# Two second products moved ahead of a kv product, and one x product moved ahead of an h product, in a fused attention and feed-forward kernel

## The chip, the cores and the metric

One core of a Trainium2 chip. The metric is the device time of one execution in microseconds (us), median over executions. Every position below is in us from the start of the profiled execution of the kernel named. The engines are called PE (matmuls; PEld are its weight loads), ACT (ScalarE), DVE (VectorE), POOL (GpSimd) and SP (issues most DMAs). The granted clock is the share of PE's full clock that it was given. All timed runs quoted are "fast" (here: not over 1.5% above the fastest run of the same kernel), apart from one single run.

## The reference, cut to what matters

```python
# q, k, v: 8 batches, 8 heads, 576 positions, 64 wide
q_s = softmax(q, axis=-1); k_s = softmax(k, axis=2)
kv   = einsum('bhsd,bhse->bhde', k_s, v)        # "kv product"
x    = einsum('bhsd,bhde->bhse', q_s, kv)       # "x product", 4608 x 512 in all
h = x @ w_in                                    # "h product", 512 -> 2048
s = sin(alpha * h)
g = h + s * s / (alpha + 1e-09)
out = g @ w_out                                 # "second product", 2048 -> 512
```

## The kernel before

Tokens go through in nine blocks t of 512; a batch has 576 tokens, so the attention of later batches is woven between the products of earlier blocks. On each engine instructions run in the order of the program. An h product is four matmuls (L248), a second product's step is one (L268), each 512 columns wide. `take(os, n)` issues the next n second-product matmuls. The first place of the change is in batch 1:

```python
        cast_v(1, [ACT_CP, DVE_CP])      # v to bf16: first half on ACT, second on DVE
        exp_to(A["qe", 1][:, 7:J], q78)
        take(os, 3)
        kv_mm(1, 0, ps_e, split=True)    # first kv product: needs v's first half
        kv_norm(1, 0, 1)
        take(os, 3)
        kv_mm(1, 1, ps_e, split=True)
        kv_norm(1, 1, 2)
        take(os, 1)
        ...                              # two x products, each followed by take(os, 2)
        take(os)                         # what is left of the 64
        ...                              # then the h products of t=1
```

The second is in block t=2, whose h products carry the attention of batch 3 between them:

```python
    def attn_out(b, ii, half, pool, eng):            # one x product and its copy to xT
        ...
        xp = pool.tile([128, 2, 512], F32, name="xp", tag="a")   # pool ps_a: one buffer
        for e in range(2):
            nc.tensor.matmul(xp[:, e, 0:n], kt[:, e, ii], qT[...], start=True, stop=True)
        c0 = (J * b + j0) * P
        eng(xT[:, 2 * ii:2 * ii + 2, c0:c0 + n], xp[:, :, 0:n])

    def attn_back(b, n, engs=(DVE_CP, DVE_CP), xs=(4, 6, 8, 10)):
        if n == 0:
            ...                                      # the kv products of batch b
        elif n in xs:
            m = xs.index(n)
            attn_out(b, m // 2, m % 2, ps_a, engs[m % 2])
    ...
    for ni in range(nN):                             # 16 h products
        h_slot(2, ni, SQ2[ni], lag, lent)            # h product, sine (ACT), square (ACT or POOL)
        flush(lag, 2)                                # g (DVE), two behind
        attn_back(3, ni - 5, (DVE_CP, ACT_CP), (5, 7, 9, 10))
```

I call the h products h0 to h15, and batch 3's four x products x0 to x3. They follow h10, h12, h14 and h15; x0 and x2 are copied by DVE, x1 and x3 by ACT, and all four use one PSUM buffer (PSUM holds what matmuls write; the pool `ps_a` has one tile of it).

The softmax here doesn't subtract the row's maximum and nothing guards it: scores larger than these inputs give would overflow.

Of the kernel before, what the change touches and what calls it, by code (L numbers as in the profile page):

```python
# [23 lines left out]
def kernel(  # L24
# [52 lines left out]
    def src_view(t, b):  # L77
        return t[b].rearrange("(i e) (p j) d -> (e p) i (j d)", e=2, j=J)
# [7 lines left out]
    def load(name, t, b, halves=False, eng=nc.sync, gate=None):  # L86

        st = stage.tile([128, 4, J, D], F32, name=f"st_{name}", tag="st")
        for ii in range(2) if gate else ():
            gate(st[:, ii, 0, 0:1], zero)  # L90
        view = src_view(t, b)
        flat = st.rearrange("p i j d -> p i (j d)")
        if halves:
            for ii in range(2):
                eng.dma_start(out=flat[:, ii::2], in_=view[:, ii::2])
        else:
            eng.dma_start(out=flat, in_=view)
        staged[name, b] = st

    def load_batch(b):  # L100
        load("q", q, b)
        load("k", k, b)
        load("v", v, b)
# [6 lines left out]
    def load_wout(c):  # L110
        nc.gpsimd.dma_start(out=wout[:, 4 * c:4 * c + 4, :], in_=wout_v[:, 4 * c:4 * c + 4, :])
# [4 lines left out]
    def exp_to(dst, src, iis=range(2)):  # L116
        for ii in iis:
            nc.scalar.activation(dst[:, :, ii * 128:(ii + 1) * 128].rearrange("p j (x d) -> p x j d", x=2),  # L118
                                 src[:, ii::2], AX.Exp)
# [5 lines left out]
    def exp_half(name, b, ii, j1=J):  # L125
        if ii == 0:
            A[name + "e", b] = att2.tile([128, J, 4 * D], BF16, name=name + "e")
        exp_to(A[name + "e", b][:, 0:j1], staged[name, b][:, :, 0:j1], (ii,))

    def exp_k(b):  # L130
        A["ke", b] = att2.tile([128, J, 4 * D], BF16, name="ke")
        exp_to(A["ke", b], staged["k", b])
# [22 lines left out]
    def norm_late(b, j0):  # L155

        qe = A["qe", b][:, j0:J].rearrange("p j (i d) -> p j i d", i=4)
        qs = small.tile([128, J, 4], F32, name="qs")[:, j0:J]
        nc.vector.tensor_reduce(qs, qe, axis=AXL.X, op=ALU.add)
        nc.vector.reciprocal(qs, qs)  # L160
        nc.vector.tensor_tensor(qe, qe, qs.unsqueeze(3).to_broadcast([128, J - j0, 4, D]), op=ALU.mult)
# [25 lines left out]
    def q_tile(b):  # L187
        if ("qT", b) not in A:
            A["qT", b] = att2.tile([128, 2, J, 128], BF16, name="qT")
        return A["qT", b]  # L190
# [6 lines left out]
    def q_transpose_ii(b, ii, j0, j1, tp):  # L197

        for j in range(j0, j1):
            nc.tensor.transpose(tp[:, j - j0], A["qn", b][:, ii, j], identb)  # L200
# [24 lines left out]
    def attn_chunk(b, c, j0, j1, xp):  # L225

        ii, e = divmod(c, 2)
        nc.tensor.matmul(xp, kbd[b % 2][:, e, ii], A["qT", b][:, ii, j0:j1, e * 64:(e + 1) * 64],
                         start=True, stop=True)
# [51 lines left out]
    ACT_CP, DVE_CP, GP_CP = nc.scalar.copy, nc.vector.tensor_copy, nc.gpsimd.tensor_copy  # L281
# [4 lines left out]
    def load0(eng, n, t, ii, j0=0, j1=J):  # L286
        eng.dma_start(out=staged[n, 0][:, ii::2, j0:j1].rearrange("p i j d -> p i (j d)"),
                      in_=src_view(t, 0)[:, ii::2, j0 * D:j1 * D])
# [80 lines left out]
    def h_slot(t, ni, sq, lag, wide=None):  # L369
        hp = mm_h(t, ni, wide, 2 if t < 2 and ni < 2 else 0)  # L370
        lag.append((t, ni, hp, sine(t, ni, hp, sq)))

    def flush(lag, keep):
        while len(lag) > keep:
            combine(*lag.pop(0))

    def o_quad(t, accs, engs):

        R = range(4)
        by_m, by_n = [(n, m) for m in R for n in R], [(n, m) for n in R for m in R]  # L380
        orders = [by_m, by_n, by_n, by_m]
        for c in R:
            for n, m in orders[c]:
                mm_o(t, m, 4 * c + n, accs[m])
                if c == 3 and n == 3:
                    evac_o(t, m, accs[m], engs[m])
                yield

    def take(it, n=1000):
        for _ in range(n):  # L390
            if next(it, 0) == 0:
                return
# [4 lines left out]
    with ES:  # L397
        def lent():
            return ps_e.tile([128, 2, MF], F32, name="hh", tag="a")[:, 0]

        def load_q8():
            for ii in range(2):
                load0(nc.sync, "q", q, ii, 8, 9)

        def load_q1():
            staged["q", 1] = st = stage.tile([128, 4, J, D], F32, name="st_q", tag="st")
            for ii in range(2):
                DVE_CP(st[:, ii, 0, 0:1], zero)
            for ii in range(2):
                nc.sync.dma_start(out=st[:, ii::2, 0:7].rearrange("p i j d -> p i (j d)"),  # L410
                                  in_=src_view(q, 1)[:, ii::2, 0:7 * D])

        late = {4: load_q8, 6: load_q1, 8: lambda: load_wout(2),
                10: lambda: load_wout(3), 13: lambda: load("k", k, 1, halves=True, gate=DVE_CP)}
        for ni in range(nN):
            h_slot(0, ni, "DPPAPPAPPPAPPAPP"[ni], lag, lent)
            flush(lag, 1)
            if ni in late:
                late[ni]()
        flush(lag, 0)  # L420

        accs = [ps_h.tile([128, dm], F32, name="hp", tag="h") for _ in range(4)]
        os = o_quad(0, accs, [DVE_CP, ACT_CP, DVE_CP, DVE_CP])
        take(os, 46)
        exp_to(A["qe", 0][:, 8:9], staged["q", 0][:, :, 8:9])
        for ii in range(2):
            exp_half("q", 1, ii, 7)
        load("v", v, 1, halves=True)
        nc.sync.dma_start(out=q78.rearrange("p i j d -> p i (j d)"), in_=src_view(q, 1)[:, :, 7 * D:J * D])
        load_batch(2)  # L430
        norm_late(0, 8)
        norm_q(1, [GP, V], 7)
        exp_k(1)
        q_tile(1)
        for ii in range(2):
            tp = ps_e.tile([128, 16, 128], BF16, name="tp", tag="a")
            q_transpose_ii(1, ii, 0, 7, tp)
            if ii == 1:
                for i2 in range(2):
                    nc.tensor.transpose(tp[:, 8 + i2], A["qe", 0][:, 8, i2 * 128:(i2 + 1) * 128], identb)  # L440
            DVE_CP(A["qT", 1][:, ii, 0:7], tp[:, 0:7])
        DVE_CP(A["qT", 0][:, :, 8], tp[:, 8:10])
        take(os, 6)
        xp = ps_e.tile([128, 4, P], F32, name="xp", tag="a")
        for c in range(4):
            attn_chunk(0, c, 8, 9, xp[:, c])
        DVE_CP(xT[:, :, 8 * P:9 * P], xp)
        cast_v(1, [ACT_CP, DVE_CP])
        exp_to(A["qe", 1][:, 7:J], q78)
        take(os, 3)  # L450
        kv_mm(1, 0, ps_e, split=True)
        kv_norm(1, 0, 1)
        take(os, 3)
        kv_mm(1, 1, ps_e, split=True)
        kv_norm(1, 1, 2)
        take(os, 1)

        c0 = J * P
        for ii in range(2):
            xp = ps_e.tile([128, 2, 512], F32, name="xp", tag="a")[:, :, 0:7 * P]  # L460
            for e in range(2):
                attn_chunk(1, 2 * ii + e, 0, 7, xp[:, e])
            (ACT_CP, DVE_CP)[ii](xT[:, 2 * ii:2 * ii + 2, c0:c0 + 7 * P], xp)
            if ii == 0:
                nc.scalar.activation(zero, zero, AX.Sin)
            take(os, 2)
        take(os)
        norm_late(1, 7)
        load("q", q, 3)
        load("k", k, 3)  # L470

        for ki in range(2):
            for ni in range(2):
                mm_h(1, ni, lent, ki, ki + 1)
        for ni in range(nN):
            h_slot(1, ni, SQ[ni], lag, lent)
            flush(lag, 1)
        cast_v(2, [GP_CP, GP_CP])
        flush(lag, 0)
# [17 lines left out]
    os = o_stream(1)  # L497
# [40 lines left out]
    def attn_back(b, n, engs=(DVE_CP, DVE_CP), xs=(4, 6, 8, 10)):  # L538
        if n == 0:
            kv_mm(b, 0, ps_a)  # L540
            kv_mm(b, 1, ps_a)
            kv_norm(b)
# [3 lines that stand above are left out]
# [5 lines left out]
    for ni in range(nN):  # L551
        h_slot(2, ni, SQ2[ni], lag, lent)
        flush(lag, 2)
        attn_back(3, ni - 5, (DVE_CP, ACT_CP), (5, 7, 9, 10))
    flush(lag, 0)

    for t in range(3, nT):
        b = t + 1 if t + 1 < B else None
        os = o_stream(t - 1)
# [59 lines left out]
```

## Time and profile before

| | before |
|---|---|
| median of 6 runs | 287.76 us (287.33 to 288.11) |
| profiled execution | span 285.8 us, granted clock 0.999 |
| PE busy | 95% of the span |
| PE's starts around the first kv product of batch 1 | 41.27, then 42.09 |
| h products of t=1 begin | 46.14 |
| from the first g of t=2 to h4 of t=3 | 21.95 us |

How to read it: the chain of waits says which engine's work ended last at each moment; where it is on PE, only fewer or earlier matmuls help; where it is on another engine, PE is waiting for it. The last row is a ruler. It is taken from the timelines of DVE and PE (columns: start, duration, engine, line, operation, tiles, shape, count, idle time before and what ended it). Its first end in the profile of before is this row; its other end is the h product at 103.23 that the prediction shows:

```profile
81.28 2.75 DVE L264 SCALAR_TENSOR_TENSOR g<-s,inva_sb,hp 128x512 bf16<-128x512 f32 x4
```

The ruler frees the second place of the change from whatever happened earlier in the same execution: 103.23 - 81.28 = 21.95.

### The profile page before, as it was taken

The numbers are of one execution on the slowest core, as the hardware profiler recorded it, in microseconds if no ns is written. First come the engines' busy times: TensorE is split into PE (matmuls) and PEld (weight loads), VectorE is DVE, ScalarE is ACT, GpSimd is POOL, SyncE is SP. The second block draws the span as 40 slices with busy tenths as digits, with TensorE's granted clock in tenths as the row PEclk, the third lists the DMA queues.
The fourth block names the chain that finished last, engine by engine and source line by source line (L and its number), as shares of the span: only waits on it lengthen the run. The fifth ranks groups of instructions, "written<-read, shape, count | busy, mean of one in ns | idle before, by whom it ended". The sixth has DMA issues, their size and how long they took to land.

```text
span 285.8 us, 4247 instructions
## 1 busy us (share of the span) xinstructions
PE 272.6 (95%) x1541; PEld 130.8 (46%) x1569; DVE 192.6 (67%) x291; ACT 226.0 (79%) x321; POOL 80.6 (28%) x75
## 2 busy tenths in 40 slices
PE   2899999999999999999999999999999999999994
PEld 1444454445454454444544454445444444444443
DVE  4857967999999658766785677667674555555321
ACT  4898748999489999899889988998877777777400
POOL 2869512773477480005300530041000000000000
PEclk9999999999999999999999999999999999999999
DMA  7999999843999984139711990016011111111242
GB/s 261 308 204 243 260 397 407 312 169 78 275 222 412 372 169 105 37 69 406 218 38 39 359 292 20 22 36 155 1 39 37 37 37 39 37 38 41 46 100 73
DMA packets 38581, 45.77 MB, mean 160 GB/s; under 512 B 16528, under 2 KB 22432, under 8 KB 38560
## 3 DMA queue, kind: packets, MB, share of 16 engines
q1 hardware_dynamic: 33376, 40.57, 46.3%
q0 software_dynamic: 4992, 4.79, 9.7%
q8 instruction: 12, 0.20, 0.3%
q10 hardware_dynamic: 192, 0.14, 0.2%
q14 instruction: 9, 0.07, 0.1%
HBM read 36.71 MB, written 9.44 MB: 161 GB/s over the span
## 4 chain that ended last, share of the span: by engine, by line
PE 74%; DVE 9%; DMA 7%; ACT 4%; issue 3%; POOL 2%; SPq 0%; ACTq 0%
PE op L268 33%; PE hp L248 33%; DMA st_v<-in_v_dram 5%; ACT s L254 3%; DVE g L264 2%; POOL s L258 2%; PE kvp L171 2%; DVE qs L150 2%; PE xp L220 2%; DMA st_q<-in_q_dram 1%; PE op L589 1%; PE hh L248 1%; DVE vb L137 1%; DVE qn L152 1%; DVE kbd L184 1%
## 5 line engine op out<-in xcount | busy, mean ns | idle before, releaser
L264 DVE SCALAR_TENSOR_TENSOR g<-s,inva_sb,hp 128x512 bf16<-128x512 f32 x130 | 96.0, 745 | 58.4 <-ACT s L256 54.2
L248 PE MATMUL hp<-xT,win 128*128 128x512 bf16 x512 | 129.0, 379 | 0.5
L268 PE MATMUL op<-wout,g 128*128 128x512 bf16 x479 | 121.9, 379 | 1.2 <-issue 0.6
L254 ACT ACTIVATE s<-hp,alpha_sb 128x512 f32<-128x512 f32 x130 | 87.8, 682 | 25.1 <-PE hp L248 22.6
L248 PEld LDWEIGHTS <-win 128*128 128x128 bf16 x576 | 56.3, 98 | 67.5 <-issue 0.8
L268 PEld LDWEIGHTS <-g 128*128 128x128 bf16 x560 | 54.1, 98 | 61.1 <-issue 0.4
L256 ACT ACTIVATE s<-s 128x512 f32<-128x512 f32 x111 | 69.9, 630 | 3.5
L152 POOL TENSOR_TENSOR qn<-qe,qs 128x1152 bf16<-128x1152 bf16 (+1 forms) x12 | 24.9, 2091 | 78.6 <-DVE qs L146 69.2
L258 POOL TENSOR_TENSOR s<-s 128x512 f32<-128x512 f32 x30 | 33.0, 1111 | 22.3 <-ACT s L254 22.0
L274 DVE COPY o<-op 128x512 f32<-128x512 f32 (+2 forms) x33 | 22.0, 668 | 9.7 <-PE op L268 5.8
L118 ACT ACTIVATE ke<-st_k 128x1152 bf16<-128x1152 f32 x16 | 17.9, 1151 | 5.0 <-DMA st_k<-in_k_dram 5.0
L118 ACT ACTIVATE qe<-st_q 128x1152 bf16<-128x1152 f32 (+3 forms) x18 | 17.7, 1025 | 2.1 <-DMA st_q<-in_q_dram 1.9
L145 DVE TENSOR_REDUCE qs<-qe 128x36 f32<-128x2304 bf16 x5 | 12.8, 2553 | 8.7 <-ACT qe L118 8.6
L268 PE MATMUL hp<-wout,g 128*128 128x512 bf16 x62 | 14.8, 379 | 0.2 <-issue 0.2
L223 DVE CAST xT<-xp 128x512 bf16<-128x512 f32 (+1 forms) x18 | 13.4, 742 | 0.0
L137 POOL CAST vb<-st_v 128x1152 bf16<-128x1152 f32 x10 | 11.3, 1163 | 6.5 <-DMA st_v<-in_v_dram 6.5
L171 PEld LDWEIGHTS <-ke 64*128 64x128 bf16 x288 | 8.4, 93 | 4.9 <-issue 1.9
L171 PE MATMUL kvp<-vb,ke 64*128 64x130 bf16 x288 | 9.9, 216 | 0.7 <-ACT vb L137 0.4
L118 ACT ACT_TABLE_LOAD x7 | 9.0, 1283 | 1.3 <-PEq L603 1.2
L248 PE MATMUL hh<-xT,win 128*128 128x512 bf16 x39 | 9.6, 379 | 0.1
L220 PE MATMUL xp<-qT,kbd 128*128 128x256 bf16 (+1 forms) x40 | 8.2, 286 | 0.4 <-DVE xT L223 0.3
L150 DVE TENSOR_REDUCE qs<-qe 128x16 f32<-128x1024 bf16 (+2 forms) x6 | 7.2, 1197 | 1.8 <-ACT qe L118 1.8
(79 smaller groups left out, 123.1 us busy)
## 6 DMA issues: line engine op xcount, KB each, us to landing
out_dram<-o SPq DMA_DIRECT2D x70, 128.0 KB, 2.3
st_q<-in_q_dram SPq DMA_DIRECT2D x6, 1152.0 KB, 6.7
st_k<-in_k_dram SPq DMA_DIRECT2D x6, 1152.0 KB, 8.9
st_v<-in_v_dram SPq DMA_DIRECT2D x6, 1152.0 KB, 10.2
st_k<-in_k_dram SPq DMA_DIRECT2D x4, 576.0 KB, 7.1
wout<-in_moe_w_out_dram POOLq DMA_DIRECT2D x4, 512.0 KB, 11.7
st_v<-in_v_dram SPq DMA_DIRECT2D x3, 576.0 KB, 9.4
win<-in_moe_w_in_dram POOLq DMA_DIRECT2D x6, 256.0 KB, 7.7
```

The lines of the kernel that those rows point to most:

```text
L118: nc.scalar.activation(dst[:, :, ii * 128:(ii + 1) * 128].rearrange("p j (x d) -> p x j d", x=2), src[:, ii::2], AX.Exp)
L137: engs[ii](vv[:, 2 * ii:2 * ii + 2, :, 0:D], staged["v", b][:, ii::2])
L152: engs[ii % len(engs)].tensor_tensor(qn[:, ii, 0:j1].rearrange("p j (x d) -> p j x d", x=2), qe[:, ii], part.unsqueeze(3).to_broadcast([12 ...
L171: nc.tensor.matmul(kvp[:, e, ii * 130:(ii + 1) * 130], ke[r, j, ii * 128:(ii + 1) * 128], vt[r, j, ii * 130:(ii + 1) * 130], start=(j == 0 ...
L220: nc.tensor.matmul(xp[:, e, 0:n], kt[:, e, ii], qT[:, ii, j0:j1, e * 64:(e + 1) * 64], start=True, stop=True)
L248: nc.tensor.matmul(hp, win[:, ki, ni * 128:(ni + 1) * 128], xT[:, ki, t * MF:(t + 1) * MF], start=(ki == 0), stop=(ki == 3))
L254: nc.scalar.activation(s, hp, AX.Sin, scale=alpha_sb[:, ni:ni + 1])
L256: nc.scalar.activation(s, s, AX.Square)
L258: nc.gpsimd.tensor_tensor(s, s, s, op=ALU.mult)
L264: nc.vector.scalar_tensor_tensor(G[t][:, ni], in0=s, scalar=inva_sb[:, ni:ni + 1], in1=hp, op0=ALU.mult, op1=ALU.add)
L268: nc.tensor.matmul(acc, G[t][:, ni, j * 128:(j + 1) * 128], wout[:, ni, :], start=(ni == 0), stop=(ni == nN - 1))
L274: eng(o[:, cols], acc)
```

## The change

The intent, as the diff reads: fill PE's wait before the first kv product of batch 1 with two matmuls that stood behind it, and take the two last x products of batch 3 apart, so that the last need not wait for the copy of the one before.

```diff
-        take(os, 3)
+        take(os, 5)
         kv_mm(1, 0, ps_e, split=True)
         kv_norm(1, 0, 1)
-        take(os, 3)
+        take(os, 2)
         kv_mm(1, 1, ps_e, split=True)
@@
-        attn_back(3, ni - 5, (DVE_CP, ACT_CP), (5, 7, 9, 10))
+        attn_back(3, ni - 5, (DVE_CP, ACT_CP), (5, 7, 8, 10))
```

Part A is the first, part B the second. The prediction works out what each does to the order of the instructions.

## The prediction

> **What bounds the kernel now.** I read the page first, then the chain of waits in order of time, then the timeline of each engine around the two places that the diff touches. All times are microseconds from the start of the profiled execution (span 285.8; timed median 287.75).
>
> ```profile
> PE 272.6 (95%) x1541; PEld 130.8 (46%) x1569; DVE 192.6 (67%) x291; ACT 226.0 (79%) x321; POOL 80.6 (28%) x75
> PE 74%; DVE 9%; DMA 7%; ACT 4%; issue 3%; POOL 2%; SPq 0%; ACTq 0%
> ```
>
> The first line is busy time by engine, the second the shares of the chain that ended last. TensorE (PE) carries three quarters of the chain, so as a whole the kernel is bound by its matmul stream; the other quarter lies before 105 us. The two changed places lie there, one in a stretch bound by PE, the other in one bound by ScalarE (ACT).
>
> Place A, the middle of batch 1, from PE's timeline:
>
> ```profile
> 40.84 0.81 PE L268 MATMUL hp<-wout,g 128*128 128x512 bf16 x3
> 42.09 0.69 PE L171 MATMUL kvp<-vb,ke 64*128 64x130 bf16 x18 [0.44 <-ACT vb L137]
> ```
>
> Three second products (the g times w_out matmuls, L268) run; then PE idles until ACT has cast the first half of v (40.87 to 42.05), and the first kv product begins at 42.09.
>
> Place B, the end of block t=2, where the x products of batch 3 (L220) stand between the h products (L248). First PE's timeline, then ACT's:
>
> ```profile
> 89.40 0.43 PE L220 MATMUL xp<-qT,kbd 128*128 128x320 bf16 x2
> 89.67 1.89 PE L248 MATMUL hp<-xT,win 128*128 128x512 bf16 x8
> 91.39 0.38 PE L220 MATMUL xp<-qT,kbd 128*128 128x256 bf16 x2
> 91.61 1.03 PE L248 MATMUL hp<-xT,win 128*128 128x512 bf16 x4
> 92.92 0.43 PE L220 MATMUL xp<-qT,kbd 128*128 128x320 bf16 x2 [0.28 <-DVE xT L223]
> ```
>
> ```profile
> 89.70 0.67 ACT L254 ACTIVATE s<-hp,alpha_sb 128x512 f32<-128x512 f32 x1
> 90.27 0.68 ACT L223 CAST xT<-xp 128x640 bf16<-128x640 f32 x1
> 90.84 1.44 ACT L254 ACTIVATE s<-hp,alpha_sb 128x512 f32<-128x512 f32 x2
> 92.31 0.63 ACT L256 ACTIVATE s<-s 128x512 f32<-128x512 f32 x1
> ```
>
> PE waits before the last x product, but ACT is packed here: each row starts as the one before ends. What this stage costs the end is decided 10 us later, where ACT's queue meets PE again:
>
> ```profile
> 102.43 0.75 DVE L264 SCALAR_TENSOR_TENSOR g<-s,inva_sb,hp 128x512 bf16<-128x512 f32 x1 [1.80 <-ACT s L256]
> 103.23 1.02 PE L248 MATMUL hp<-xT,win 128*128 128x512 bf16 x4
> ```
>
> The fifth h product of t=3 needs the PSUM buffer of the first, freed by that g at 103.18, and starts at 103.23. PE's own stream would have reached it at 103.11 (two matmuls from 102.68, 0.216 each), so PE loses 0.12 there. After it I find no irregular gap in PE's starts until the end, apart from missing records and four regular kv switches: the end is fixed by this start.
>
> **What the Trainium skill says.** (1) "TensorE: Matmul & The Clock Gate", Back-to-back issue gap: N/2.4 + 2.5 ns when warm, 215.8 ns for N = 512. The trace agrees: starts at 40.841, 41.058, 41.274, and the granted clock is full in all slices. (2) "TensorEngine Tiling (Array Packing)", Key Properties: a change of tiling mode drains the engine. It agrees: from the last 128-row matmul to the first 64-row kv matmul the trace has 0.312 instead of 0.216, at 43.46, 67.40 and 81.70. (3) "PSUM — Partial Sum Buffer", Engine vs sequencer instructions: ScalarE and VectorE queues are strict FIFO, matmuls start in program order. The argument on place B rests on this, and the rows agree. (4) "Perfetto Trace Analysis", DVE / Act Engine Instruction: the propagation of a semaphore lies outside the shown duration. Here a release costs 0.055 (g ends 103.178, matmul starts 103.230).
>
> **The change, part by part.** It adds and removes no work; the built programs differ in order alone. Part A moves two L268 matmuls from behind the first kv product to before it: one from between the two kv products, one from the very end of the block. Part B moves batch 3's third x product one h product forward, from after h14 to after h13, and its DVE copy one g forward. ACT, POOL and the DMA queue keep their orders.
>
> Part A. Gap in starts before kv: 0.816 (41.274 to 42.090); a switch needs 0.312, so 0.504 is removable. Two matmuls of 0.216 fill 0.432. The first kv product could then start at 42.02, still waits for the cast, and keeps its 42.09. Behind it PE has two matmuls fewer before t=1's h products: 2 x 0.216 = 0.43 less. Checks on what could take its place: the second kv product would start at 43.25 instead of 43.46; its v half is cast by 43.07. The copy of the first x product to xT moves from 44.88 to 44.67 and ends near 45.58, before h at 45.71. The second, on DVE, is the tight one: its product ends at 45.44, the copy runs 45.48 to 46.56, the fifth h matmul can start at 46.615, PE reaches it at 46.57, so 0.04 is lost. Net -0.39. From 46.1 to 60.1 PE is packed (64 x 0.216 = 13.8), and what follows (exponentials, norm, the transposes, the load of v for batch 3 issued at 71.84 and landing at 78.09, its cast to 81.36) hangs on it link by link, so I carry -0.39 through.
>
> Part B, in the old times (all shift alike). There is one PSUM buffer for x products. The third, moved up, reaches PE at 90.53 (h13 is 4 x 0.216 from 89.67) but needs the copy of the second, on ACT, which ends at 90.948. It starts at 91.00: a new wait of 0.47. Its two matmuls take 0.216, so h14 starts at 91.22 instead of 90.53, +0.69. ACT's sine of h14 started at 91.595, 0.04 after h14's end, so it moves to 92.29. ACT has nothing else to run, and from there its queue is serial: square, sine of h15, copy of the fourth x product, table load, four exponentials, table load, first sine of t=3, square; all +0.69. PE gains its old wait before the fourth x product, because the DVE copy is now done early (about 92.1), and reaches that product at 92.95 against 92.92: nothing won. The g that frees the PSUM buffer ends 0.69 later, so h4 of t=3 starts at 103.92 instead of 103.23.
>
> Sum: -0.39 + 0.69 = +0.30; 287.75 + 0.30 = 288.05, which I round to 288.0.
>
> **Rivals.** First, part B costs nothing and A alone shows: -0.39, so 287.35. For it: PE is the bound over the whole kernel and the visible PE wait of 0.28 goes away; an author would move it for that. Against it: ACT has no slack from 90.8 to 101.7, and the copy it now waits for is on record at 90.95. Second, A is swallowed on the way: the load of v at 71.84 could take longer or a DVE copy take the place of the cast as the wait; then B stands alone, +0.69, 288.45. For it: the chain has a 6.25 load in it, whose length depends on other traffic. Against: its issue follows the work before. Third, both work as intended, A's 0.39 and B's removed PE wait (0.45 from 92.47 to 92.92): 286.9. Against: the 0.12 at 103.11 is all that PE could win, since h4 waits for ACT.
>
> **Range and chances.** My main path gets about 0.6, the first rival 0.2, the rest share what is left. The runs of before spread by 0.78 (287.33 to 288.11), more than the effect. That gives 287.2 to 288.6. Two per cent is 5.8 us; nothing in either part, with all its waits, reaches 1 us. So within 2% gets 0.98.
>
> **What would show it right or wrong.** Part A right: the wait before the first kv product falls from 0.44 to near zero with five L268 matmuls ahead, kv still starts near 42.09, the h products of t=1 start at 45.7 instead of 46.14, and the cast of v at 77.7 instead of 78.11. Part B right: a gap in PE after h13 ended by ACT's xT copy; about 0.7 of ACT idle before the sine of h14; the distance from the cast of v (78.11) to h4 of t=3 (103.23), 25.1 now, grows to 25.8. It is wrong if that distance stays or shrinks, if ACT's copy of the second x product comes before 90.5 on this scale, or if PE waits again after 103.

## The result, and the profile after

The changed kernel took 288.36 us (median of 6 runs, 287.81 to 288.63) against 287.76: the ratio is 1.002, with an interval of 1.0006 to 1.0033, so it is slower by 0.17 to 0.95 us. A ratio is the mean time of one kernel's fast runs over that of the other's of the same rounds, so not quite the ratio of the medians.

The two lines of the page that answer to those of before, busy time and shares of the chain:

```profile
PE 273.1 (95%) x1541; PEld 131.0 (46%) x1569; DVE 193.5 (67%) x291; ACT 225.9 (79%) x321; POOL 80.0 (28%) x75
PE 80%; DVE 7%; ACT 4%; DMA 4%; issue 2%; SPq 1%; ACTq 0%
```

The counts are the same, and DMA's share of the chain fell from 7% to 4%. What left it is seen in the chain in order of time (start, duration, what). First before, then after, each around the first kv product of batch 1:

```profile
31.44 9.41 DMA st_v<-in_v_dram
40.87 1.18 ACT vb L137
42.09 0.69 PE kvp L171 x18
```

```profile
41.58 0.12 PE xp L228 x4
41.70 1.08 PE hp L268 x5
42.77 0.62 PE kvp L171 x18
```

In the execution of before the kv product came out of the load of v. In that of after it came out of PE's own work: PE got there late. PE's timeline of the changed kernel at place A:

```profile
41.53 1.24 PE L268 MATMUL hp<-wout,g 128*128 128x512 bf16 x5
42.71 0.68 PE L171 MATMUL kvp<-vb,ke 64*128 64x130 bf16 x18
...
46.33 1.03 PE L248 MATMUL hp<-xT,win 128*128 128x512 bf16 x4
```

Five matmuls stand ahead and there is no wait, as predicted, but the three that were there before began at 41.53 instead of 40.84, 0.69 later, and the kv product at 42.71 instead of 42.09. The h products of t=1 began at 46.33, not at the predicted 45.7, and even 0.19 later than before. That delay is older than the change: nothing before 40 us was touched. It goes back to the start of the execution. ACT's timeline there, before and after:

```profile
7.15 1.06 ACT L118 ACTIVATE qe<-st_q 128x1024 bf16<-128x1024 f32 x1
```

```profile
7.87 1.06 ACT L118 ACTIVATE qe<-st_q 128x1024 bf16<-128x1024 f32 x1 [0.67 <-DMA st_q<-in_q_dram]
```

The exponential of the second half of batch 0's q waited 0.67 for its load in this execution and began 0.72 later. The first h product of t=0 is already 0.68 later (15.32 instead of 14.64), and PE carried that up to the kv product.

At place B, PE and then ACT in the changed kernel (this execution is 0.23 behind that of before here: its first g of t=2 is at 81.51):

```profile
81.51 2.75 DVE L264 SCALAR_TENSOR_TENSOR g<-s,inva_sb,hp 128x512 bf16<-128x512 f32 x4
```

```profile
89.63 0.43 PE L220 MATMUL xp<-qT,kbd 128*128 128x320 bf16 x2
89.90 1.02 PE L248 MATMUL hp<-xT,win 128*128 128x512 bf16 x4
91.23 0.38 PE L220 MATMUL xp<-qT,kbd 128*128 128x256 bf16 x2 [0.30 <-ACT xT L223]
91.45 1.89 PE L248 MATMUL hp<-xT,win 128*128 128x512 bf16 x8
93.17 0.43 PE L220 MATMUL xp<-qT,kbd 128*128 128x320 bf16 x2
...
104.15 1.02 PE L248 MATMUL hp<-xT,win 128*128 128x512 bf16 x4 [0.61 <-DVE g L264]
```

```profile
90.50 0.68 ACT L223 CAST xT<-xp 128x640 bf16<-128x640 f32 x1
...
92.51 0.69 ACT L254 ACTIVATE s<-hp,alpha_sb 128x512 f32<-128x512 f32 x1 [0.74 <-PE hp L248]
```

The wait before x3 (93.17) is gone, and a wait before x2 (91.23) has come, ended by ACT's copy of x1. The sine of h14 starts at 92.51 after 0.74 of idle ACT, and h4 of t=3, at 104.15, waits 0.61 for the g that frees its buffer. The ruler reads 104.15 - 81.51 = 22.64: part B cost 0.69 here, the predicted number. From h4 to the end both executions take 182.52, and all 14 profiles 182.50 to 182.54: what the ruler gains or loses reaches the end in full.

### The profile page after: what moved, and what is told of

The parts are those of the page before. It is cut to its first block, busy times and chain, and to the rows that moved or that the text cites. A ratio compares the mean times of both kernels' runs of the same rounds, so it can differ in the third digit from the quotient of the medians.

```text
span 286.7 us, 4247 instructions
## 1 busy us (share of the span) xinstructions
PE 273.1 (95%) x1541; PEld 131.0 (46%) x1569; DVE 193.5 (67%) x291; ACT 225.9 (79%) x321; POOL 80.0 (28%) x75
## 3 DMA queue, kind: packets, MB, share of 16 engines
q0 software_dynamic: 4992, 4.79, 9.6%
## 4 chain that ended last, share of the span: by engine, by line
PE 80%; DVE 7%; ACT 4%; DMA 4%; issue 2%; SPq 1%; ACTq 0%
PE hp L248 35%; PE op L268 31%; PE hp L268 5%; PE hh L248 3%; DMA st_v<-in_v_dram 2%; PE kvp L171 2%; DVE g L264 2%; DMA st_q<-in_q_dram 2%; PE xp L220 2%; DVE qs L150 1%; ACT s L254 1%; PE op L589 1%; DVE vb L137 1%; ACT qe L118 1%; ACT ke L118 1%
## 5 line engine op out<-in xcount | busy, mean ns | idle before, releaser
L268 PE MATMUL op<-wout,g 128*128 128x512 bf16 x479 | 121.8, 379 | 1.2 <-issue 0.6
L268 PEld LDWEIGHTS <-g 128*128 128x128 bf16 x560 | 54.1, 98 | 61.0 <-issue 0.4
L268 PE MATMUL hp<-wout,g 128*128 128x512 bf16 x62 | 14.8, 379 | 0.2 <-issue 0.2
```

Source lines behind the costliest of these rows:

```text
L268: nc.tensor.matmul(acc, G[t][:, ni, j * 128:(j + 1) * 128], wout[:, ni, :], start=(ni == 0), stop=(ni == nN - 1))
```

## The experiments

Twelve runs were made, all correct, on four chips; each is compared with before on its own chip in the same rounds. My theory after the result: part B costs 0.69 by ACT's queue, in every execution. Part A can only fill the time in which PE stands idle before the first kv product, and the profile of before had caught an execution with an early start, in which that time was large. The rivals are named with each run.

### The two halves, both together, and a buffer of its own for x2

`e1_A` is the first hunk of the diff alone, `e2_B` the second alone, `e3_both` the changed kernel again. `e4_B_bank` is part B with this edit, which keeps the PSUM buffer of x2 apart from that of x1:

```diff
+        if (b, ii, half) == (3, 1, 0):
+            xp = ps_o.tile([128, 2, 256], F32, name="xq", tag="o")
+        else:
             xp = pool.tile([128, 2, 512], F32, name="xp", tag="a")
```

> Part A alone (five second products ahead of the first kv product of batch 1, two behind it). Theory: A pays only as far as PE stands idle before that kv product, and that idle time depends on how late PE comes out of the start of the execution, which varies from run to run (the first sine-free exponential of q's second half began at 7.15 in the profile of before and at 7.87 in that of after). With an early start the h products of t=1 begin at 45.75 instead of 46.14 and the time falls by 0.39; with a late one (0.69) they begin near 46.35, as they would have without A, and the gain is nothing, or a loss of 0.05 for a DVE copy. Over the runs I expect -0.1 (from the measured +0.6 of both parts less the +0.69 of B), between -0.3 and +0.1. Rival: A gains its 0.39 at the h products in every run and loses it later, on the load and the cast of batch 3's v: then the h products begin 0.39 earlier than before at equal start, and the cast of v does not. The position from the cast to the fifth h product of t=3 should be that of before (first g of t=2 to that product: 21.95).

> Part B alone (third x product of batch 3 one h product earlier). Theory: from the first g of t=2 to the start of the fifth h product of t=3 22.64 instead of 21.95, as in the profile of after, with an ACT gap of 0.74 before the sine of h14; the time rises by 0.69. Rival: B costs less in time than in this stretch, because PE catches up later: then the time rises by 0.2 or less. Rival two: the whole 0.6 of both parts is chance of the start: then B is within 0.2 of before.

> The changed kernel again, on the chip of the two halves. +0.3 to +0.7 against before; if the parts do not meet, the sum of part A alone and part B alone.

> Part B alone, but the third x product (2 x 256 columns, one PSUM bank) is put into a bank of the pool of the second products, so that it need not wait for ACT's copy of the second x product. It must then wait for the g of h10, which in the profile of after ended 0.29 before that copy. Theory (the wait for the PSUM buffer held by ACT's copy is what delays h14 and then ACT): the wait shrinks by 0.29, the stretch from the first g of t=2 to the fifth h product of t=3 is 22.35, and the time is +0.40 against before instead of +0.69; the part that stays is the x product's own 0.216 and the shorter wait. Rival (the order of DVE's copy and g's, or the place of the x product alone, makes the delay): the stretch stays at 22.6.

Measured, against 287.85 of before in the same rounds (11 runs):

| run | median of 6 | ratio, 95% interval | ruler |
|---|---|---|---|
| e1_A | 287.87 | 1.0008, 0.9985 to 1.003 | 21.95 |
| e2_B | 288.73 | 1.0032, 1.0018 to 1.0046 | 22.64 |
| e3_both | 288.46 | 1.0017, 1.0004 to 1.003 | 22.64 |
| e4_B_bank | 288.38 | 1.002, 1.0006 to 1.0035 | 22.35 |

The loss comes with part B: the ratio of `e2_B` is +0.92 us (0.0032 x 287.85), and its interval (0.52 to 1.32) holds the predicted 0.69. The ruler repeats to 0.01. Part A alone changes nothing that these rounds can show; one of its six runs took 289.64 at a granted clock of 0.994, which widens the interval so far (-0.43 to +0.86 us) that it also holds the predicted -0.39. Nor is it resolved whether the parts add up: by ratios they are +0.23 and +0.92 alone and +0.49 together, and `e3_both` less `e2_B`, -0.43, would by itself look like A's full gain. What follows on the size of A rests on profiles, not on times. The rival of chance for B falls.

`e4_B_bank` moved the ruler by the 0.29 that was expected. Its x2 began at 91.56 with h13 started at 90.52 (the edit shifts line numbers by 3):

```profile
90.52 1.02 PE L251 MATMUL hp<-xT,win 128*128 128x512 bf16 x4
91.56 0.38 PE L223 MATMUL xq<-qT,kbd 128*128 128x256 bf16 x2
```

That is 1.04 after h13's start, where the changed kernel has 1.33 (91.23 - 89.90). So it is the buffer held by ACT's copy that delays x2. The rest, 22.35 against 21.95, is the 0.22 of x2's own two matmuls and 0.18 that x2 still waits (91.56 instead of 91.38, four matmuls after 90.52), as expected for the g of h10 that frees its new buffer: that g ends at 91.51.

In the profile of `e1_A` PE again waited for v even with five matmuls ahead (0.44 between starts, 0.31 is the mode switch), so A filled its whole 0.43 there. In that of `e3_both` PE would have come 1.2 later than v even with three, and A filled nothing. One kernel's profile cannot tell the worth of A.

### Part A where v is made late, and where PE is made late

Four ACT copies of no use stand ahead of the cast of v in `e5_vlate`; `e6_vlate_A` adds part A. Two DVE reductions of no use stand in the start in `e7_pelate`; `e8_pelate_A` adds part A.

```diff
# e5_vlate
+        for _ in range(4):
+            ACT_CP(spool.tile([128, MF], F32, name="s"), A["ke", 1][:, 0:2].rearrange("p j c -> p (j c)"))
         cast_v(1, [ACT_CP, DVE_CP])
# e7_pelate
+    for _ in range(2):
+        nc.vector.tensor_reduce(small.tile([128, 16], F32, name="late"), A["qe", 0][:, 0:4].rearrange("p j (i d) -> p (j i) d", i=4), axis=AXL.X, op=ALU.add)
     cast_v0(0, 0, 9, ACT_CP)
```

> The kernel before, with four copies of no use on ACT ahead of its cast of batch 1's v, so that v always comes later than PE. Both theories: PE idles by 1.0 to 2.5 before the first kv product in every run; h products of t=1 begin 4.05 after that kv product (as in before, B and the bank variant); the time rises by 1 to 2 against before.

> The same with part A. Theory (A is worth the idle time before the first kv product that it can fill, whatever the start): here the full 0.43 can be filled, the h products begin 3.62 to 3.67 after that kv product, and the time is 0.35 to 0.43 below that of the kernel without A and with the same copies. Rival (A's gain is taken back later in every run): the time is equal to it within 0.15.

> The kernel before, with two reductions of no use on DVE in the start of the execution (2.4 by their own durations), so that PE always comes later than v. PE does not wait before the first kv product (0.31 between starts, the mode switch alone); the time rises by 1 to 2.4 against before.

> The same with part A. Theory: there is nothing to fill, so A gains nothing; the DVE copy of the second x product holds the fifth h matmul by 0.05 as in both profiles of A, and the time is equal to that of the kernel without A and with the same reductions, within 0.15 (at most 0.05 longer). Rival (A gains its 0.39 in any case): 0.39 less.

PE's timelines with v late, without and with part A:

```profile
44.02 0.69 PE L171 MATMUL kvp<-vb,ke 64*128 64x130 bf16 x18 [1.56 <-ACT vb L137]
...
48.08 3.62 PE L248 MATMUL hp<-xT,win 128*128 128x512 bf16 x16
```

```profile
43.56 0.69 PE L171 MATMUL kvp<-vb,ke 64*128 64x130 bf16 x18 [0.93 <-ACT vb L137]
...
47.19 3.66 PE L248 MATMUL hp<-xT,win 128*128 128x512 bf16 x16
```

From the kv product to the h products it is 4.06 without and 3.63 with part A: 0.43 filled. Of that, some 0.05 is lost within the h products (16 matmuls in 3.66 instead of 3.62); in the program the fifth of them waits for DVE's copy of the second x product of batch 1 to xT, the one that the prediction called tight. Carried on to the first g of t=2, A's gain measured from the end of v's cast is 0.38. The rival, a loss later on, falls. The medians, 289.21 with A and 289.66 without, differ by 0.45 in the right direction; their ratios to before, 1.0068 and 1.0081, have intervals of 0.0045 and 0.0044 that overlap, so the times alone would not settle it. `e5_vlate` lost a little more to the copies than I had expected (0.0081 x 287.67 = 2.3 instead of 1 to 2).

With PE late, without and with part A:

```profile
45.65 0.81 PE L268 MATMUL hp<-wout,g 128*128 128x512 bf16 x3
46.39 0.68 PE L171 MATMUL kvp<-vb,ke 64*128 64x130 bf16 x18
...
50.45 1.89 PE L248 MATMUL hp<-xT,win 128*128 128x512 bf16 x8
```

```profile
43.09 1.24 PE L268 MATMUL hp<-wout,g 128*128 128x512 bf16 x5
44.26 0.69 PE L171 MATMUL kvp<-vb,ke 64*128 64x130 bf16 x18
...
47.88 3.67 PE L248 MATMUL hp<-xT,win 128*128 128x512 bf16 x16
```

The second is joined by ACT's row for the cast of v in the same profile:

```profile
43.00 1.17 ACT L137 CAST vb<-st_v 128x1152 bf16<-128x1152 f32 x1 [0.19 <-DMA st_v<-in_v_dram]
```

From the first of the three or five L268 matmuls to the h products it is 4.80 without and 4.79 with part A. But this pair did not test what it was meant to. In `e8_pelate_A` v's load was late too: the cast ended at 44.17, so the kv product could start at 44.22 at the earliest, and with three matmuls ahead PE would have been ready at 43.83 (44.26 less 0.43). A therefore filled 0.39 in that profile. The distance cannot show it, because it holds only matmuls once PE no longer waits. What A does where PE really is late is seen in executions without the reductions: with three ahead and PE 0.88 behind v (`e12_before`, below) the distance is 4.79 (46.80 - 42.01), with five ahead and PE even with three behind v (after, above) 4.80 (46.33 - 41.53). Nothing is gained there. The times of `e7_pelate` and `e8_pelate_A` (290.03 and 291.04) say nothing: with the reductions in the start some executions ran at granted clocks down to 0.988, in both kernels and in unequal number, and took up to 292.77. The two profiles stand 2.6 apart when they get here, and only their inner distances are compared.

### What carries part B's cost to the end, and a version built from it

`e9_B_m3` is part B with the copy of x3 on DVE. `e11_bank_m3` is the kernel before, with x2 in a buffer of its own (edit above) and x3's copy on DVE; `e10_best` adds part A.

```diff
-            attn_out(b, m // 2, m % 2, ps_a, engs[m % 2])
+            attn_out(b, m // 2, m % 2, ps_a, DVE_CP if (b, m) == (3, 3) else engs[m % 2])
```

> Part B alone, and the copy of the fourth x product of batch 3 on DVE instead of ACT. PE's wait before the third x product stays as it is. Theory (what B costs is carried to the end by ACT's serial queue, not by PE's own wait): ACT's table load follows the sine of h15 at once, 0.58 earlier, so the stretch from the first g of t=2 to the fifth h product of t=3 is 22.06 instead of 22.64, and the time is +0.1 against before (-0.1 to +0.4). Rival (PE's wait is the cost): the stretch stays at 22.6 and the time at +0.7.

> Old place of the blocks, part A, the third x product in a PSUM bank of its own, the fourth copy on DVE. Theory: neither the third nor the fourth x product waits any more (PE wins the 0.45 before the fourth), ACT's queue is 0.58 shorter, both reach the fifth h product of t=3 at the same time; the stretch is 21.38 instead of 21.95. With part A's 0 to 0.39 the time is -0.6 to -0.9 against before. Rival (PE's wait at the fourth x product costs nothing and ACT is not the queue that decides): stretch 21.8 to 21.95, time within 0.2 of before.

> The same without part A: stretch 21.38, time -0.57 against before, and 0 to 0.39 above the run with part A according to how often PE comes before v (about 0.1 on the mean of the profiles seen so far).

Against 287.86 of before in the same rounds (11 runs):

| run | median | ratio, 95% interval | ruler |
|---|---|---|---|
| e9_B_m3 | 287.77 (5 runs) | 1.0001, 0.9989 to 1.0013 | 22.05 |
| e10_best | 287.37 (6 runs) | 0.999, 0.9969 to 1.0011 | 21.40 |
| e11_bank_m3 | 287.29 (5 runs) | 0.9981, 0.9968 to 0.9994 | 21.40 |

In `e9_B_m3` PE's wait before x2 is still there (0.30, ended by ACT's copy) and so is the idle 0.74 before the sine of h14. Yet the ruler falls from 22.64 to 22.05, because ACT's table load now follows the sine of h15:

```profile
92.42 0.69 ACT L254 ACTIVATE s<-hp,alpha_sb 128x512 f32<-128x512 f32 x1 [0.74 <-PE hp L248]
...
93.68 0.67 ACT L254 ACTIVATE s<-hp,alpha_sb 128x512 f32<-128x512 f32 x1
94.37 1.28 ACT L118 ACT_TABLE_LOAD   x1
```

So PE's wait is not itself what is paid at the end: what it costs, it costs through ACT's queue behind it.

`e11_bank_m3` beats the kernel before: 0.0019 x 287.86 = 0.55 less than before, with an interval below 1, and expected at 0.57. Its two edits were not run apart. Its x3 follows h15 without a wait, 0.87 after h15's start, where before had 1.31 (92.92 - 91.61; lines shifted by 3):

```profile
92.54 1.03 PE L251 MATMUL hp<-xT,win 128*128 128x512 bf16 x4
93.41 0.43 PE L223 MATMUL xp<-qT,kbd 128*128 128x320 bf16 x2
```

Part A on top of it (`e10_best`) brings nothing that shows: its ratio stands for 0.29 less than before where I had expected 0.6 to 0.9. One of its six runs took 289.1; its median, 287.37, is beside the 287.29 of the kernel without A.

### The kernel before, looked at again

> The kernel before once more, unchanged, for a second look at its start. Theory: the 0.50 of idle time that the prediction took from the one profile was that of an early start; in the nine profiles without an artificial delay so far, the time that part A can or could fill was 0.43, 0, 0.43, 0.06, 0, 0, 0, 0.04 and 0, so here most likely under 0.1. Rival: the wait belongs to this kernel and is 0.50 again (then the first kv product starts 0.8 after the matmul before it). In both cases 21.95 from the first g of t=2 to the fifth h product of t=3.

One run, 288.23 us (another execution of the same code beside it took 287.66), unchanged code:

```profile
42.01 0.81 PE L268 MATMUL hp<-wout,g 128*128 128x512 bf16 x3
42.76 0.69 PE L171 MATMUL kvp<-vb,ke 64*128 64x130 bf16 x18
...
46.80 0.38 PE L248 MATMUL hp<-xT,win 128*128 128x512 bf16 x1
```

No wait: PE came 1.17 after the first profile's 40.84, and v had been cast at 41.82. The 0.44 of the first profile does not belong to the kernel. This table collects all profiles without an artificial delay. "PE" is where the first kv product could start by PE alone with three matmuls ahead (last start before it + 0.312, less 0.432 where five stand ahead); "v" is the end of the cast + 0.05; the last column is what A fills or would fill, at most 0.43.

| profile | PE | v | fillable |
|---|---|---|---|
| before | 41.59 | 42.09 | 0.43 |
| after | 42.28 | 42.09 | 0 |
| e1_A | 42.37 | 42.93 | 0.43 |
| e2_B | 43.15 | 43.21 | 0.06 |
| e3_both | 42.93 | 41.74 | 0 |
| e4_B_bank | 42.94 | 42.32 | 0 |
| e9_B_m3 | 42.23 | 41.90 | 0 |
| e10_best | 42.61 | 42.65 | 0.04 |
| e11_bank_m3 | 43.02 | 42.14 | 0 |
| e12_before | 42.76 | 41.87 | 0 |

The mean is 0.10, nearly all of it from two profiles; `e1_A` to `e4_B_bank`, on one chip, differ as much as the rest. From the first h product of t=1 to the first g of t=2 these ten take 35.13 to 35.15 without A and 35.18 to 35.19 with it, so the 0.05 on DVE's copy is lost every time, and what scatters lies before. Less that 0.05, A is worth about 0.05 on average, an estimate from ten profiles.

## Why the prediction was right or wrong

The time, 288.36, lies inside the range of 287.2 to 288.6, and within 2% was right. But that says little: the range also held the first two rivals (287.35 and 288.45), the sum had +0.30 where +0.60 came, and 288.36 lies nearer to the second rival than to my 288.05. The parts fared unequally.

Part B was right step by step. Set back by the 0.23 by which the profile after trails, x2 starts at 91.00 (predicted 91.00), the sine of h14 at 92.28 (92.29), and h4 of t=3 at 103.92 (103.92). The queue that was to carry it was tested in `e9_B_m3`, the buffer in `e4_B_bank`. The marker that I had named for it, from the cast of v to h4, grew from 25.12 to 25.64 only, not to 25.8: the cast began with another wait and ran shorter (3.09 instead of 3.25), so a later row, the first g, was the better end of a ruler.

In part A the mechanism was right and the size off. The step that failed is "Gap in starts before kv: 0.816 (41.274 to 42.090); a switch needs 0.312, so 0.504 is removable", and with it "Net -0.39". The gap was real, but it was one execution's. Over ten profiles the fillable part is 0.10 on average, and the net about -0.05. `e6_vlate_A` shows the predicted 0.43 where v is late; after and `e12_before`, where PE is late, take the same time with A and without. With A's size so estimated and B's measured the sum is -0.05 + 0.69 = +0.64; measured 288.36 - 287.76 = +0.60. The times are too coarse to confirm A's part of it.

One small reading of the prediction is off: its own numbers for the release (103.178 to 103.230) give 0.052, not 0.055; nothing turns on it.

The rivals: that B costs nothing fell (`e2_B`). That A would be swallowed came true, but not on the way that I gave it: nothing took it back at the load of batch 3's v, it was missing before it began. That both gain fell with the first. The profiled execution of before had been a warning that I did not use: it took 287.56, below the median of 287.75, and a wait that is the difference of two arrivals, a load and an engine, moves with both.

What stays open: why PE's and v's arrivals vary. The start of the second exponential of q lies between 7.09 and 8.57 in these profiles, and waits for loads are part of it, but in `e9_B_m3` it was early and PE lost its 0.6 a little later. In seven of the ten profiles of the table PE's first L268 matmul of the three or five follows that exponential by 33.66 to 33.77; in `e2_B`, `e3_both` and `e9_B_m3` another 0.4 to 0.7 was lost between. I did not follow that to its cause.

## What to carry to other kernels

Before filling a wait that hangs on a load, look at it in several executions: what counts is the mean of the part that can be filled, not the wait in one profile. When a wait of one engine is removed by moving work, ask which buffer the moved work needs and which engine's queue frees it; here PE had made up its own wait by x3, and the 0.69 that ACT then fell behind was paid in full. A ruler between two fixed instructions, both behind the noisy start, resolved 0.01 us where timed runs scattered by 0.8.

## What the Trainium skill lacked or had wrong

- "TensorE: Matmul & The Clock Gate", Back-to-back issue gap: it gives 131 ns per matmul as the sustained figure for N = 512 with weight loads between, and says that the formula with 216 ns over-counts there. Here 64 such matmuls, each with its weight load, take 13.8 us in t=1: 0.216 each, the formula's figure.
- "TensorEngine Tiling (Array Packing)", Key Properties: it says that a change of tiling mode drains the engine, but gives no duration. Here the entry into 64-row mode puts 0.312 between starts instead of 0.216, so 0.096 more, in every such switch after 40 us at which PE waits for nothing else.
- "Perfetto Trace Analysis", DVE / Act Engine Instruction: it tells that the propagation of a semaphore is outside the shown duration, without a figure. Here PE's matmul starts 0.050 to 0.058 after the end of the DVE or ACT instruction that releases it (92.865 to 92.920 behind a copy, 103.178 to 103.230 behind a g, both in the kernel before).
- No page that I read tells how far the first loads of an execution scatter: the second exponential of q, which needs one of them, began between 7.09 and 8.57 in profiles of kernels with the same start.
